# Scaling the half tiles between two layers on ScalarE instead of GpSimd, and holding their transposes back less

## The chip, the cores and the metric

One NeuronCore of a Trainium2 chip runs the kernel. The metric is device time in microseconds (us). The engines are named as in the profile: PE is TensorE, PEld its weight loads, DVE is VectorE, ACT is ScalarE, POOL is GpSimd, SP is the engine whose queue issues the DMAs.

## What is computed

Three steps in a row, all in float32 at the interface:

```
scores = (q @ k^T) / 8 * decay            # 4 x 8 heads, 576 positions, head size 64
x      = (scores @ v), laid out as 2304 x 512
P      = softmax-like gate of x, 8 rounds of row and column normalization (8 experts)
x      = sum over e of P[:, e] * (relu(x @ w1[e]) @ w2[e])       # 512 -> 1024 -> 512
h      = x @ w_in;  g = max(0.01 * h, h);  out = g @ w_out       # 512 -> 2048 -> 512
```

The matrices w_in and w_out arrive as 64-bit numbers and are turned into float32 on the chip.

## The kernel before, in words

Both feed-forward layers are cut into units of 512 hidden columns: 16 units for the eight experts (units 0 to 15), 4 for the second layer (units 16 to 19). Each unit runs over the tokens in three stages of 384 tokens per half (the 2304 tokens are two halves of 1152; tile j is 128 tokens, and tile j of the first half goes with tile j of the second; j runs from 0 to 8). Within a unit the product is done by a fast scheme of seven block products in place of eight, and each operand is a pair of 16-bit parts, high and low, so that three matmuls stand for one. The first products of a stage (`product_h`, L996) are interleaved by hand with the second products of an earlier stage (`group_s`, L1167; for units 0 and 15 the plain form, L1209). PE is given this order.

What the other engines do beside it is put in order while the program is built, by the class `Order`. It keeps a planned time `t` of PE and a planned time at which each engine comes free. Tasks stand in queues (evac, turn, gate, hid, weights, f64). After each few matmuls `tick` calls `pump`, which goes through the queues in this order and issues each task that is ready. A task with several engines ("AD": ACT or DVE) goes to the one that the plan has free the longest. The price of a task is `a + b * n` for n elements: on ACT 0.2 + 0.00089 n, on DVE 0.17 + 0.00105 n, on POOL 0.28 + 0.0020 n. `lat` is how long after the planned end of what it needs a task is held back:

```
L92   return (all(d.done is not None and d.done + x.lat <= self.t + 0.25 for d in x.deps)
L93           and (x.cond is None or x.cond()) and (not x.eng or min(self.free[e] for e in x.eng) <= self.t + SLACK))
```

The engines' own queues run in the order of issue; a task that the plan issues too early makes its engine wait on a semaphore, and with it all that is queued behind.

When a tile pair j of unit 15 is finished (`close`, L1190), it becomes an operand of the second layer; this is the turn (`turn_steps`, L1279). For each of the two half tiles (128 x 512) of the pair: a sum of absolute values (`sums`, L1289 on ACT or L1291 on DVE), then for both together a power of two for each row (`norms`, four small DVE instructions: L155, L156, L1299, L161), the scaling of the half tile in place by it (`scaled`, L1306), four PE transposes of 128 x 128 into a PSUM bank (`turned`, L1316), and a copy of that bank to SBUF on ACT or DVE (L63). `operand_tasks` then forms sums of blocks on POOL (`sums_a`, `sums_b`, L501 to L508), takes the 16-bit high parts (L63) and low parts (DVE, L530) and writes four pieces for each pair to DRAM from SP's queue (L455), from where the stages of the second layer load them into a ring (L479). There are 9 pairs, so 18 scalings, 72 transposes and 36 pieces.

In the same stretch the weights of units 16 and 17 are prepared: magnitudes (ACT, L197), high parts (ACT, L250 and L279), low parts and block differences (POOL, L260, L267, L285). The raw weights of the next unit (`load_raw`, L182) are asked for when the last of these is done and no piece is outstanding (`landed`, L173).

Of the kernel before, what the change touches and what calls it, by code (L numbers as in the profile page):

```python
# [13 lines left out]
AF = mybir.ActivationFunctionType  # L14
ALU = mybir.AluOpType
# [46 lines left out]
def copy_on(e, out_, in_):  # L62
    (e.copy if e is nc_of["A"] else e.tensor_copy)(out_, in_)  # L63
# [62 lines left out]
def retention_moe_ffn_kernel(ctx: ExitStack, tc: tile.TileContext, qk, vk, wg, wm, wf,  # L126
                             c_dt, c_gq, c_gk, c_id, out):
    nc = tc.nc
# [23 lines left out]
    def pow2(out_, in_, name):  # L152

        t = small.tile(list(out_.shape), F32, tag=f"pw{out_.shape[-1]}", name=f"pw{name}", bufs=2)
        nc.vector.tensor_scalar(t, in_, 2.0 ** -90, None, op0=ALU.max)  # L155
        nc.vector.tensor_scalar(out_.bitcast(I32), t.bitcast(I32), EXPM, EXPM,  # L156
                                op0=ALU.bitwise_xor, op1=ALU.bitwise_and)

    def recip2(out_, in_):

        nc.vector.tensor_scalar(out_.bitcast(I32), in_.bitcast(I32), -1.0, float(254 << 23),  # L161
                                op0=ALU.mult, op1=ALU.add)
# [394 lines left out]
    def idle_bank(name):  # L557

        return s1[1 - last_pair[0] % 2]
# [334 lines left out]
    y = [ypool.tile([P, DM], F32, name=f"y{i}") for i in range(2 * NJ)]  # L894
# [241 lines left out]
    def group_s(u, s, jj, what):  # L1136
# [53 lines left out]
        def close():  # L1190
            if jj == NT_S - 1:
                s_done.add((u, s))
            if u == NU1 - 1:
                turn_steps(s, j)
# [84 lines left out]
    def turn_steps(s, j0):  # L1279

        xs, st = {}, {}

        def sums(j, h):
            def f(e):
                if h == 0:
                    st["l", j] = small.tile([P, 2], F32, tag="l1", name=f"tl1{j}")
                i, o = y[h * NJ + j], st["l", j][:, h:h + 1]
                if e is nc.scalar:
                    nc.scalar.activation(junk, i, AF.Abs, accum_out=o)  # L1289
                else:  # L1290
                    nc.vector.tensor_reduce(o, i, axis=AX.X, op=ALU.add, apply_absolute_value=True)  # L1291
            return f

        def norms(j):
            def f():
                s1 = small.tile([P, 2], F32, tag="ts1", name=f"ts1{j}")
                s2 = st["s", j] = small.tile([P, 2], F32, tag="s2", name=f"ts2{j}")
                pow2(s1, st["l", j], f"t{j}")
                nc.vector.tensor_scalar(s2, s1, XS, None, op0=ALU.mult)  # L1299
                recip2(inv.rearrange("p (h j) -> p h j", h=2)[:, :, j], s1)  # L1300
            return f

        def scaled(j, h):
            def f():
                i = h * NJ + j
                nc.gpsimd.tensor_scalar(y[i], y[i], st["s", j][:, h:h + 1], None, op0=ALU.mult)  # L1306
            return f

        xt = [None, None]

        def turned(j, h):
            def f(e):
                i = h * NJ + j
                ptv = idle_bank(f"xt{i}").rearrange("p (k i) -> p k i", k=NP)
                for k in range(NP):
                    nc.tensor.transpose(ptv[:, k, :], y[i][:, 128 * k:128 * k + 128], ident)  # L1316
                xt[h] = wtmp.tile([P, NP, P], F32, tag="r64", name=f"tx{i}", bufs=R64)
                copy_on(e, xt[h], ptv)
            return f

        j, p, key = j0, turn_last, (1, s)

        def add(eng, n, f, deps, lat=LAT):
            x = Task(eng, n, f, tuple(d for d in deps if d), key, None, lat)
            order.queues["turn"].append(x)
            return x

        y_done = Task(None, 0, None, done=max(order.free["D"], order.free["A"]))
        a = [add("AD", 512, sums(j, h), (y_done,)) for h in range(2)]
        a = add("D", 300, norms(j), a)  # L1330
        b = [add("G", 512, scaled(j, h), (a,)) for h in range(2)]
        t = [add("AD", 512, turned(j, h), (b[h],) + p.get(f"x{h}", ()), 1.5) for h in range(2)]
        operand_tasks(1, j, xt, tuple(t), key, p)

    gates = []
# [160 lines left out]
```

## Time and profile before

| | |
|---|---|
| median of 3 runs | 1814.27 us (1813.0 to 1817.39) |
| profiled execution, span from first to last instruction | 1814.0 us |
| PE busy | 1780.4 us, 98% |
| DVE busy | 1484.6 us, 82% |
| ACT busy | 1260.0 us, 69% |
| POOL busy | 823.9 us, 45% |
| POOL, scaling of the half tiles (L1306) | 18 instructions, 33.3 us, from 1390 to 1486 us |

The profile is of one execution. A busy share is an average over the whole span; the turn takes place between about 1388 and 1500 us, and the rows of that stretch are what the change is read from. Small idle times of PE are listed in the trace by what ended them. Matmuls are pipelined, so a matmul row is longer than the distance to the next.

### The profile page before, as it was taken

To read this page: it belongs to the slowest core of one execution; us is meant where nothing else is said; L and a number is where in the kernel's file an instruction comes from. 1 tells how busy PE (TensorE), PEld (TensorE's weight loads), DVE (VectorE), ACT (ScalarE), POOL (GpSimd) and SP (SyncE) were. 2 spreads that over 40 slices of the span, in tenths; PEclk is the share of its full clock that TensorE was granted. 3 is DMA by queue.
4 is the path that set the end of the run, shared out by engine and by line. 5 is a ranking of instruction groups with operands and counts; after the bars stand their busy time and mean duration, and the time that the engine had idled before them with its cause. 6 is when DMAs were issued, how large, how long until landed. Compare 5 with 4: busy or idle time off the path is not lost.

```text
span 1814.0 us, 35903 instructions
## 1 busy us (share of the span) xinstructions
PE 1780.4 (98%) x13800; PEld 1294.5 (71%) x13800; DVE 1484.6 (82%) x2583; ACT 1260.0 (69%) x2657; POOL 823.9 (45%) x782
## 2 busy tenths in 40 slices
PE   8999999999999999999999999999999989999998
PEld 7755577777777777777777777777776556777776
DVE  7955989988888887888888888878875896788876
ACT  5776776767676677767676767777675667876753
POOL 4815452626344453626263444536234882443610
PEclk9999999999999999999999999999999999999999
DMA  9773445446354454454453544544443444435242
GB/s 339 272 250 102 144 139 169 141 137 186 112 172 126 147 161 137 133 171 133 139 186 107 176 124 154 163 132 133 152 129 114 160 156 146 129 104 159 79 128 82
DMA packets 206784, 272.99 MB, mean 150 GB/s; under 512 B 13698, under 2 KB 177556, under 8 KB 201492
## 3 DMA queue, kind: packets, MB, share of 16 engines
q1 hardware_dynamic: 206612, 270.70, 47.7%
q8 instruction: 108, 1.77, 0.4%
q14 instruction: 64, 0.52, 0.1%
HBM read 241.02 MB, written 29.63 MB: 149 GB/s over the span
## 4 chain that ended last, share of the span: by engine, by line
PE 89%; DVE 5%; DMA 2%; POOL 1%; ACT 1%; issue 1%; SPq 0%; DVEq 0%; POOLq 0%; ACTq 0%
PE s L1167 17%; PE hB L996 13%; PE hA L996 12%; PE hE L996 12%; PE s1a L1167 12%; PE s1b L1167 11%; PE hD L996 6%; PE s L1209 2%; DMA qk<-in_qk 1%; PE s1a L1209 1%; PE s1b L1209 1%; DVE xst L530 1%; DMA xring<-x 1%; POOL y L1306 1%; DVE hs L1087 0%
## 5 line engine op out<-in xcount | busy, mean ns | idle before, releaser
L996 PEld LDWEIGHTS <-w 128*128 128x128 f16 x5040 | 491.4, 98 | 260.9 <-issue 6.8
L1167 PEld LDWEIGHTS <-hs 128*128 128x128 f16 x3888 | 379.4, 98 | 88.5 <-DVE hs L1087 5.2
L260 POOL TENSOR_TENSOR w<-raw,w 128x384 f16<-128x384 f32 x152 | 168.8, 1128 | 384.7 <-ACT w L250 384.4
L1167 PEld LDWEIGHTS <-hp 128*128 128x128 f16 x2916 | 285.4, 98 | 79.9 <-issue 1.9
L267 POOL TENSOR_TENSOR raw<-raw 128x256 f32<-128x256 f32 x304 | 281.6, 926 | 19.9
L1180 DVE SCALAR_TENSOR_TENSOR y<-s,fac,y 128x256 f32<-128x256 f32 (+1 forms) x322 | 197.5, 614 | 105.9 <-PE s L1167 89.3
L996 PE MATMUL hE<-xring,w 128*128 128x384 f16 x1440 | 276.3, 327 | 3.4 <-POOL w L285 1.8
L996 PE MATMUL hB<-xring,w 128*128 128x384 f16 x1440 | 276.4, 327 | 0.4 <-ACT hB L1006 0.4
L996 PE MATMUL hA<-xring,w 128*128 128x384 f16 x1440 | 274.8, 327 | 0.0
L1167 PE MATMUL s<-w,hs 128*128 128x256 f16 x1932 | 263.7, 273 | 0.0
L1087 DVE TENSOR_TENSOR hs<-fs,hs 128x768 f16<-128x768 f32 (+1 forms) x228 | 240.3, 1057 | 7.4 <-ACT hs L1077 6.4
L285 POOL TENSOR_TENSOR w<-raw,w 128x512 f16<-128x512 f32 x148 | 201.9, 1379 | 72.6 <-ACT w L279 72.4
L1077 ACT ACTIVATE hs<-fs 128x768 f16<-128x768 f32 (+1 forms) x228 | 187.6, 823 | 46.8 <-DVE fs L1112 38.2
L415 POOL TENSOR_TENSOR f<-f,e 128x256 f32<-128x256 f32 x64 | 52.9, 826 | 343.3 <-DVE e L407 343.3
L1077 ACT ACTIVATE hp<-fp 128x384 f16<-128x384 f32 x240 | 160.6, 678 | 13.0 <-DVE fp L1035 12.0
L1180 DVE SCALAR_TENSOR_TENSOR y<-s1a,fac,y 128x256 f32<-128x256 f32 (+1 forms) x161 | 98.8, 614 | 59.0 <-ACT s L1185 32.8
L1167 PE MATMUL s1a<-w,hs 128*128 128x256 f16 x972 | 133.5, 273 | 4.6 <-ACT hs L1077 2.4
L996 PE MATMUL hD<-xring,w 128*128 128x384 f16 x720 | 136.8, 326 | 1.1 <-ACT hD L1024 1.1
L1180 DVE SCALAR_TENSOR_TENSOR y<-s1b,fac,y 128x256 f32<-128x256 f32 (+1 forms) x161 | 98.6, 613 | 46.8 <-PE s1b L1167 20.5
L1167 PE MATMUL s1b<-w,hs 128*128 128x256 f16 x960 | 132.2, 274 | 2.3 <-DVE hs L1087 1.9
L1167 PE MATMUL s1a<-w,hp 128*128 128x256 f16 x972 | 132.6, 273 | 1.0 <-DVE y L1180 1.0
L1167 PE MATMUL s<-w,hp 128*128 128x256 f16 x966 | 131.8, 273 | 0.0
(213 smaller groups left out, 2683.0 us busy)
## 6 DMA issues: line engine op xcount, KB each, us to landing
xring<-x SPq DMA_DIRECT2D x413, 384.0 KB
raw<-in_wm SPq DMA_DIRECT2D x32, 1024.0 KB
r<-in_wf SPq DMA_DIRECT2D x64, 256.0 KB
qk<-in_qk SPq DMA_DIRECT2D x16, 512.0 KB
vk<-in_vk SPq DMA_DIRECT2D x16, 512.0 KB
wf_s<-f SPq DMA_DIRECT2D x32, 256.0 KB
raw<-wf_s SPq DMA_DIRECT2D x8, 1024.0 KB
x<-xst SPq DMA_DIRECT2D x30, 256.0 KB
```

The costliest lines, as they stand in the source:

```text
L260: nc.gpsimd.tensor_tensor(v[0], v[1], v[2], op=ALU.subtract)
L267: nc.gpsimd.tensor_tensor(o, x, y_, op=ALU.subtract)
L285: (nc.gpsimd if u or part else nc.vector).tensor_tensor(lo, r, hi, op=ALU.subtract)
L415: nc.gpsimd.tensor_tensor(dst, dst, cur["tx"].bitcast(F32), op=ALU.mult)
L530: nc.vector.tensor_tensor(st[d][:, :, 1], src[d](), st[d][:, :, 0], op=ALU.subtract)
L996: nc.tensor.matmul(bank, w[:, a, wi, k, :], x[:, :, b, k, :], start=r in (1, 5) and k == q == 0, stop=k == 1 and q == 2, skip_group_check= ...
L1077: nc.scalar.activation(hid[k][:, 0, a:b], src[:, a:b], AF.Relu if moe and relu else AF.Copy)
L1087: nc.vector.tensor_tensor(t[:, 1, a:b], src[:, a:b], t[:, 0, a:b], op=ALU.subtract)
L1167: nc.tensor.matmul(out_, t[:, a, i, ts], w[:, b, wi, 0, :], start=start and k == 0, stop=k == 5, skip_group_check=True)
L1180: nc.vector.scalar_tensor_tensor(out_, bank, f, out_, op0=ALU.mult, op1=ALU.add)
L1209: nc.tensor.matmul(bank, t[:, a, i, ts], w[:, b], start=l == g == q == 0, stop=l == g == 1 and q == 2, skip_group_check=True)
L1306: nc.gpsimd.tensor_scalar(y[i], y[i], st["s", j][:, h:h + 1], None, op0=ALU.mult)
```

## The change

The scaling of a half tile is issued on ACT (an activation "copy" with a factor for each partition) instead of POOL, and the plan books it on ACT at 0.656 us instead of on POOL at 1.304 us. The transposes of a half tile are held back 0.5 us instead of 1.5 us after the planned end of the scaling. Nothing else is edited; but since the order of all later tasks follows from the plan, other tasks can change their place or their engine.

```diff
         def scaled(j, h):
             def f():
                 i = h * NJ + j
-                nc.gpsimd.tensor_scalar(y[i], y[i], st["s", j][:, h:h + 1], None, op0=ALU.mult)
+                nc.scalar.activation(y[i], y[i], AF.Copy, scale=st["s", j][:, h:h + 1])
             return f
...
         a = add("D", 300, norms(j), a)
-        b = [add("G", 512, scaled(j, h), (a,)) for h in range(2)]
-        t = [add("AD", 512, turned(j, h), (b[h],) + p.get(f"x{h}", ()), 1.5) for h in range(2)]
+        b = [add("A", 512, scaled(j, h), (a,)) for h in range(2)]
+        t = [add("AD", 512, turned(j, h), (b[h],) + p.get(f"x{h}", ()), 0.5) for h in range(2)]
         operand_tasks(1, j, xt, tuple(t), key, p)
```

## Rows read from the trace of the kernel before

**Rows 1.** Page, part 1: busy time, share of the span, instructions of each engine.

```profile
PE 1780.4 (98%) x13800; PEld 1294.5 (71%) x13800; DVE 1484.6 (82%) x2583; ACT 1260.0 (69%) x2657; POOL 823.9 (45%) x782
```

**Rows 2.** Windows: stretch, length, busy us (instructions) by engine, granted clock, DMA.

```profile
800.00:1380.00 580.00, 580.00 (x4426) 431.42 (x4425) 480.81 (x832) 410.11 (x861) 254.91 (x243) 1.00 0.47 143
1380.00:1541.00 161.00, 149.64 (x911) 90.52 (x910) 129.07 (x214) 105.71 (x224) 105.00 (x94) 0.98 0.47 151
```

**Rows 3.** PE's waits, 1380 to 1540 us: total us, times, longest us.

```profile
PE s1a L1167 <- ACT hs L1077: 2.2, 1, 2.2
PE s1a L1316 <- POOL y L1306: 2.0, 3, 1.7
PE hE L996 <- POOL w L285: 1.8, 2, 1.0
PE s1a L1167 <- DVE hs L1087: 1.5, 1, 1.5
PE s1b L1316 <- POOL y L1306: 1.2, 1, 1.2
PE hD L996 <- ACT hD L1024: 1.1, 1, 1.1
```

**Rows 4.** Windows of the turn, the two stretches at the lower clock last.

```profile
1388.00:1500.00 112.00, 103.66 (x598) 59.71 (x596) 95.99 (x160) 72.39 (x156) 88.95 (x78) 0.98 0.48 160
1440.00:1487.00 47.00, 40.11 (x227) 22.10 (x226) 44.79 (x71) 29.54 (x61) 45.09 (x40) 0.99 0.53 177
...
1486.50:1489.90 3.40, 3.40 (x15) 2.24 (x14) 3.40 (x7) 2.21 (x5) 0.00 (x0) 0.53 0.21 75
...
1537.30:1541.00 3.70, 3.70 (x17) 2.40 (x18) 2.69 (x3) 1.70 (x4) 3.33 (x4) 0.54 0.00 0
```

**Rows 5.** Groups on POOL, 1388 to 1500 us: busy us, mean ns, idle before.

```profile
L1306 POOL TENSOR_SCALAR y<-y,ts 128x512 f32<-128x512 f32 x18 | 33.3, 1860 | 7.8 <-DVE inv L161 6.1 <-ACT w L279 1.1 <-DVE ts L1299 0.4
```

**Rows 6.** Groups on ACT, 1388 to 1500 us.

```profile
L63 ACT COPY tx<-s1b 128x512 f32<-128x512 f32 x7 | 4.1, 586 | 4.5 <-PE s1b L1316 4.4
...
L63 ACT COPY tx<-s1a 128x512 f32<-128x512 f32 x6 | 3.5, 585 | 5.9 <-PE s1a L1316 5.9
...
L235 ACT ACTIVATE raw<-raw,sw 128x512 f32<-128x512 f32 x4 | 2.9, 721 | 0.0
```

**Rows 7.** Timeline of DVE: the last norms before the scaling, of three pairs.

```profile
1426.16 0.17 DVE L1299 TENSOR_SCALAR ts<-ts 128x2 f32<-128x2 f32 x1
...
1436.52 0.17 DVE L1299 TENSOR_SCALAR ts<-ts 128x2 f32<-128x2 f32 x1
...
1462.74 0.58 DVE L1299 TENSOR_SCALAR ts<-ts 128x2 f32<-128x2 f32 x1
```

**Rows 8.** Timeline of PE: the first transposes of the same three pairs.

```profile
1428.28 0.60 PE L1316 MATMUL s1a<-ident,y 128*128 128x128 f32 x4
...
1438.58 0.60 PE L1316 MATMUL s1b<-ident,y 128*128 128x128 f32 x4
...
1465.11 0.66 PE L1316 MATMUL s1b<-ident,y 128*128 128x128 f32 x4 [1.24 <-POOL y L1306]
```

**Rows 9.** Timeline of POOL: one pair's scalings.

```profile
1401.34 4.17 POOL L1306 TENSOR_SCALAR y<-y,ts 128x512 f32<-128x512 f32 x2 [1.20 <-DVE inv L161]
```

**Rows 10.** Groups on DVE, 1388 to 1500 us.

```profile
L530 DVE TENSOR_TENSOR xst<-sa,xst 128x512 f16<-128x512 f32 x9 | 8.1, 905 | 0.0
L530 DVE TENSOR_TENSOR xst<-tx,xst 128x512 f16<-128x512 f32 x9 | 8.0, 893 | 0.0
L530 DVE TENSOR_TENSOR xst<-sb,xst 128x512 f16<-128x512 f32 x9 | 7.3, 809 | 0.1
...
L63 DVE COPY tx<-s1a 128x512 f32<-128x512 f32 x3 | 2.1, 692 | 2.2 <-PE s1a L1316 2.2
```

**Rows 11.** Timeline of DVE while the scalings of Rows 9 ran.

```profile
1402.14 0.68 DVE L530 TENSOR_TENSOR xst<-sb,xst 128x512 f16<-128x512 f32 x1
```

**Rows 12.** Timeline of SP's queue: the load of unit 17's second raw weights.

```profile
1481.66 0.40 SPq L182 DMA_DIRECT2D raw<-wf_s  x1
```

## The prediction

> **What bounds the kernel now.** I read first the page's busy times: PE is busy 98% of the span [rows 1], so only what lets PE stand, or slows its clock, can be won. Next the windows, to see where PE stands: from 800 to 1380 us it never does; in the 161 us from 1380 to 1541, which hold the turn and its aftermath, it is busy 149.6 us, so it stands for 11.4 us [rows 2]. In two places there its granted clock is at half (1.2 GHz instead of 2.4): 3.4 us after the stand at 1482 to 1486, and about 3.4 us after the one at 1535 to 1537 [rows 4]. Half speed for 3.4 us costs 1.7 us each time. Together 11.4 + 3.4 = 14.8 us are all that this stretch can give back, 0.8% of the span.
>
> Then PE's waits in that stretch [rows 3], for who ends the stands. Only 2.0 + 1.2 = 3.2 us end with the instruction that the change moves (POOL's scaling, L1306). 2.2 + 1.5 = 3.7 us end with the high and low parts of the hidden values of unit 16 (ACT and DVE), 1.8 us with a weight part on POOL, 1.1 us with ACT's copy to hD.
>
> Last the windows and groups of the turn, to see which engine is behind. From 1440 to 1487 us DVE is busy 44.8 of 47 us and POOL 45.1, ACT only 29.5 [rows 4]. So two engines are full there, not one. POOL has 33.3 us of scalings among 89.0 us of work from 1388 to 1500 [rows 4, 5]; DVE has none.
>
> **The change, part by part.** The sum is made against the profiled execution, 1814.0 us from first to last instruction; the median of the runs is 0.3 us above it, which I add at the end.
>
> *The scaling itself.* Removed from POOL: 18 instructions of 1.86 us, 33.3 us [rows 5]. Added to ACT: 18 of the nearest form in this stretch, the scaling of raw weights (L235), same shape, types and a factor for each partition: 0.72 us [rows 6], 18 x 0.72 = 13.0 us, which lifts ACT from 72.4 to 85.4 of 112 us. For a pair, norms to scaled tiles falls from 3.7 us (4.2 where both stand in a row, [rows 9]) to 1.4.
>
> *The transposes.* In the plan the first scaling of a pair ends 1.30 - 0.66 = 0.65 us earlier and the hold is 1.0 us shorter, so they stand 1.65 us earlier in PE's queue; the second half's 2 x 0.65 + 1.0 = 2.3 us earlier. The scaled tile is really there 1.86 - 0.72 = 1.1 us earlier for the first, 2.3 for the second. So the second keep their distance, but the first lose 0.5 us of it: PE is asked earlier than the data come. What then counts is DVE, whose norms come before the scaling. In the third pair from [rows 7, 8] PE comes to the transposes at 1463.87 (1465.11 less its 1.24 us idle), 0.55 us after the norms ended (1462.74 + 0.58 = 1463.32); in the other two 1.95 and 1.89 us after. Of the nine pairs these three are the tightest; the others have 2.4 us or more in the same views. Less 1.65, that is 0.30, 0.24 and -1.10 us, where 0.8 is needed (0.72 and two hand-overs). PE would wait 0.5, 0.6 and 1.9, together 3.0 us; with 0.3 us in ACT's queue for each, 3.9. This replaces 3.2 us. Term: +0.7 us. Bounds: -3.2 (all waits gone, if DVE gets ahead) and +8.5 (all of the last six pairs as the tightest: 6 x 1.95 = 11.7, less 3.2).
>
> *The wait added on ACT.* ACT now waits for DVE's norms; POOL did so for 6.1 us [rows 5]. Behind a waiting scaling stand ACT's evacuations of the first products (hB, p, u, fp, hD), and behind them PE. Today ACT has a third of its time free and PE waits 1.1 us for such a copy [rows 3]. Lower bound 0, upper bound all the added 13.0 us; I take 0.8 us, near the one wait that the rows show. Term: +0.8.
>
> *The wait for hD.* The 1.1 us [rows 3] stand at the end of a stretch of the chain of waits: scalings until 1405.5 [rows 9], transposes, their copy, four block sums on POOL, a cast on ACT that waits for them, and behind it in ACT's queue the copy to hD. With the scalings done about 2.8 us earlier the chain ends before PE asks. Term: -1.1; bounds -1.1 and 0.
>
> *The end of the turn.* The 3.7 us for the hidden values of unit 16, with 1.7 us of clock behind them, come from DVE, which is still busy with the pieces. Does the change unload DVE? Two things oppose. (1) Copies: with ACT booked for the scaling just before, the plan sends more "AD" work to DVE. Now ACT makes 7 + 6 = 13 of the 18 copies of transposes [rows 6] and DVE 5; I expect some five more on DVE, at 0.69 us each [rows 10]: +3.5 us. (2) DVE's instructions are longer while POOL works: the 27 wide low parts mean 0.87 us [rows 10], against 0.68 for one that ran beside a scaling without loss [rows 11]. Under the scalings of [rows 9] there is none of that excess, over all of the stretch it is 0.19 us a low part; I estimate about 0.35 us for a pair, so 9 x 0.35 = 3 us go with the scalings. (1) and (2) cancel; what remains is that each pair's pieces begin 1 to 2 us earlier, so less of the last two pairs lies in front of the hidden values. I take half of the 3.7: -1.8, and keep the clock drop. Bounds: -5.4 (stand and clock both gone) and +3.5 (the copies come, the relief does not).
>
> *The weights of unit 17.* Their second raw load is issued at 1481.66 us [rows 12], behind the writes of the pieces in SP's queue, which wait for DVE, and after unit 16's last weight parts on POOL, between the scalings. A POOL freed of 33.3 us ends those sooner; the 36 piece writes move up with the pairs, by 1 to 2 us. The load then starts a little earlier, and the 1.8 us wait for L285 shrinks. Term: -0.9 (half); bounds -3.5 (wait and clock drop gone) and 0.
>
> Sum: +0.7 + 0.8 - 1.1 - 1.8 - 0.9 = -2.3 us, so 1811.7; with the 0.3 us to the median **1812 us**.
>
> One rule of the Trainium skill bears on (2). "SBUF — State Buffer", section "Who interferes with whom", says that a DVE instruction with two SBUF inputs and a GpSimd one that reads SBUF exclude each other for a whole instruction. By it taking scalings off POOL would free DVE more than the 3 us; the trace disagrees in part: the low part of [rows 11] has two SBUF inputs and ran at its shortest in the middle of the scalings of [rows 9]. What it would give is the first rival.
>
> **Rivals.** *DVE comes free.* The 27 wide low parts last 8.1 + 8.0 + 7.3 = 23.4 us [rows 10]; at 0.68 they would last 18.4, so 5 us of DVE are lost to POOL in these alone, and half as much again in the narrow ones and the norms would make about 8. If most of it went with the scalings, DVE would be ahead by the end: the 3.2, the 3.7 with 1.7 of clock, and the 1.1 would go, less 0.8 on ACT: 8.9 us, 1805. For it: DVE and POOL are both full from 1440 to 1487 [rows 4]. Against: the rest of POOL's work, 55.6 of 89.0 us, stays, and DVE's excess is small under the scalings.
>
> *PE is asked too early: slower.* The place is PE's queue in front of the transposes of the last six pairs; the price is the difference between when DVE's norms are ready and when PE arrives, now without the 1.65 us. It decides from the point where the mean wait for a pair exceeds 3.2 / 9 = 0.36 us. If DVE lags in each of the last six pairs as it does in the tightest, PE waits 11.7 instead of 3.2 us, a third clock drop adds 1.7, and none of the later terms comes: 1814.3 + 8.5 + 1.7 = 1824. For it: DVE is 95% busy there [rows 4], and further copies may go to it. Against: each stand of PE lets DVE catch up, and two of the three tightest pairs were 1.9 us clear [rows 7, 8].
>
> *The waits change only their name.* Scaling and transposes shift together, the copies sent to DVE eat the rest, and the end of the turn is as late: +0.7 + 0.8 - 1.1 = +0.4, so 1814 to 1815.
>
> **How the numbers follow.** Forecast 0.42 (its own range 1808 to 1816), DVE free 0.23, too early 0.18, only the name 0.17. A measurement of this kernel can tell about 0.3%, 5.4 us, from no change: 1808.8 and 1819.7. Faster has the first rival and 0.05 of the forecast's lower edge: 0.28. Slower is the second rival, 0.18. The rest, 0.54, is the same. The range leaves out a tenth at each side: down to 1804, just under the first rival; up to 1821, about two thirds of the way to the second.
>
> **What would show it.** Right: the waits for L1306 stand under ACT with 3 to 5 us; DVE stays over 90% busy in the second half of the turn; POOL has some 33 us less there, ACT 12 to 14 more; about half the transposes' copies are on DVE; the 1.1 us for hD is gone; the stand at 1482 us is there, but under 3 us. Wrong to the fast side: DVE's wide low parts near 0.7 us, no stand and no clock drop at the end. Wrong to the slow side: waits for the scaling above 8 us, or evacuations on ACT (L1006 to L1024) late behind a scaling that waits for DVE. If PE stands somewhere outside 1380 to 1560 us where it does not now, the plan has changed more than I assume.

## The result and the profile after

The kernel after takes 1830.38 us (median of 4 runs, 1829.72 to 1830.72) beside 1814.81 for the kernel before on the same chip: ratio 1.0086, 95% interval [1.0071, 1.010]. It is slower by 15.6 us, where I had forecast 2 us faster; the time lies above my range. The profiled execution spans 1828.9 us, against 1814.0.

Part 1 of the page, as in [rows 1]:

```profile
PE 1783.0 (97%) x13800; PEld 1294.9 (71%) x13800; DVE 1489.3 (81%) x2585; ACT 1269.1 (69%) x2677; POOL 791.7 (43%) x764
```

PE has as many instructions as before and 2.6 us more busy time; the other 12.3 us are idle time. The windows of after (stretch, length, then busy us of PE, PEld, DVE, ACT, POOL; granted clock, DMA share, GB/s):

```profile
800.00:1380.00 580.00, 580.00 (x4428) 431.63 (x4427) 481.26 (x833) 410.49 (x862) 254.34 (x243) 1.00 0.47 143
1380.00:1560.00 180.00, 157.75 (x943) 94.21 (x942) 134.02 (x217) 118.02 (x251) 75.35 (x78) 0.95 0.43 135
1388.00:1500.00 112.00, 98.78 (x535) 54.59 (x534) 94.06 (x153) 73.72 (x157) 54.19 (x56) 0.96 0.47 152
1440.00:1487.00 47.00, 40.80 (x220) 22.43 (x221) 42.25 (x62) 32.49 (x73) 27.96 (x29) 0.96 0.44 147
```

and the second stretch in the trace of before:

```profile
1380.00:1560.00 180.00, 167.65 (x1047) 103.66 (x1046) 139.09 (x231) 122.71 (x257) 109.27 (x99) 0.98 0.46 146
```

From 800 to 1380 us nothing differs [rows 2]. In the 180 us that follow PE is busy 9.9 us less, at a lower mean clock. POOL did lose its scalings (88.95 to 54.19 us in the turn, [rows 4]). ACT gained only 1.3 us there, not 13: it gave copies away, and others of its instructions fall behind 1500 us.

Who took the copies is seen in the groups of after, 1388 to 1500 us (as [rows 5, 6, 10]):

```profile
L1306 ACT ACTIVATE y<-y,ts 128x512 f32<-128x512 f32 x18 | 12.3, 714 | 7.7 <-DVE ts L1299 7.7
L530 DVE TENSOR_TENSOR xst<-tx,xst 128x512 f16<-128x512 f32 x8 | 8.9, 1116 | 0.0
L530 DVE TENSOR_TENSOR xst<-sa,xst 128x512 f16<-128x512 f32 x8 | 8.4, 1054 | 0.0
L530 DVE TENSOR_TENSOR xst<-sb,xst 128x512 f16<-128x512 f32 x8 | 6.5, 807 | 0.1
L63 DVE COPY tx<-s1b 128x512 f32<-128x512 f32 x6 | 4.2, 692 | 6.9 <-PE s1b L1316 6.8
L63 DVE COPY tx<-s1a 128x512 f32<-128x512 f32 x6 | 4.1, 689 | 5.1 <-PE s1a L1316 3.2 <-ACT w L279 1.9
```

Twelve of the transposes' copies are on DVE; before it had five. In front of these twelve DVE stands for 6.9 + 5.1 = 12.0 us, mostly until PE's transposes are done. Before it stood 5.1 us in front of its five, 2.2 for the three in [rows 10] and 2.9 for the other two:

```profile
L63 DVE COPY tx<-s1b 128x512 f32<-128x512 f32 x2 | 1.4, 691 | 2.9 <-ACT p L1010 1.5 <-PE s1b L1316 1.3
```

In return DVE has two of the sums (L1291, 0.67 us each) instead of six. And its wide low parts did not get shorter without the scalings beside them: (8.9 + 8.4 + 6.5) / 24 = 0.99 us, against 0.87. In this window there are 24 of them instead of 27: the last pair's pieces fall behind 1500 us. (All 27 take 26.4 us, before 23.5.) The delay is plainest in SP's queue, before (first fence; start, us, instructions merged) and after:

```profile
1488.42 10.20 SPq L455 DMA_DIRECT2D x<-xst  x6
1498.72 31.46 SPq L479 DMA_DIRECT2D xring<-x  x14
```

```profile
1488.11 0.38 SPq L182 DMA_DIRECT2D raw<-wf_s  x1
1494.24 13.64 SPq L455 DMA_DIRECT2D x<-xst  x4
1508.05 0.53 SPq L479 DMA_DIRECT2D xring<-x  x1
1509.75 0.32 SPq L455 DMA_DIRECT2D x<-xst  x1
1510.18 5.19 SPq L479 DMA_DIRECT2D xring<-x  x7
```

The last piece (L455) leaves 11 us later, at 1509.75 instead of 1498.3. PE's waits of after, 1380 to 1560 us, answer to [rows 3]:

```profile
PE s1b L1316 <- ACT y L1306: 4.1, 2, 2.9
PE s1a L1167 <- ACT hs L1077: 3.2, 1, 3.2
PE s1a L1316 <- ACT y L1306: 3.2, 3, 1.7
PE hE L996 <- ACT w L279: 2.9, 1, 2.9
PE s1b L1167 <- DVE hs L1087: 1.8, 1, 1.8
PE hA L996 <- ACT w L250: 1.2, 1, 1.2
PE hE L996 <- DMA xring<-x: 1.2, 1, 1.2
...
PE hA L996 <- POOL w L260: 0.9, 1, 0.9
PE hA L996 <- DMA xring<-x: 0.7, 1, 0.7
PE s1a L1167 <- DVE hs L1087: 0.6, 1, 0.6
```

Three things grew: the scalings (7.3 us, 3.2 before), the hidden values of unit 16 (5.6, 3.7 before), the weights of unit 17 (L250, L260, L279 and 0.4 on L285: 5.4, 1.8 before); the ring loads (1.9) are new, and the 1.1 us for hD is gone. Behind the stands the clock is at 0.50 for longer, 17.0 us in three stretches instead of 6.8 in two [rows 4]:

```profile
1466.20:1469.60 3.40, 2.73 (x10) 1.88 (x11) 2.38 (x4) 3.17 (x6) 0.00 (x0) 0.50 0.93 251
1493.50:1500.30 6.80, 5.85 (x25) 3.73 (x24) 3.74 (x10) 4.32 (x10) 0.00 (x0) 0.50 0.11 40
1548.10:1554.90 6.80, 3.84 (x14) 1.72 (x15) 2.97 (x3) 3.85 (x8) 5.46 (x7) 0.50 0.00 0
```

PE was busy for 12.4 us of them, against 7.1 before; half of the difference, 2.7 us, is the cost. PE's order of products (L996, L1167, L1209) is the same in every kernel here, so the same product can be found in two traces. Its **lag** is its start less its start before, less that difference for the product at 1381.5 us, where the change has not begun. In after the lag is +5.7 at the product that started at 1486.5 us in before, +8.8 at 1502, +10.8 at 1532 (the first of unit 17), +14.6 at 1542 and +14.5 at 1599: 5.7 us in the turn, 5.1 at its end, 3.8 at unit 17's weights, nothing later. Stands of PE from the product at 1381.5 to the one at 1599 are 23.6 us against 12.8, so idle time makes 10.9 of it, the clock some 2.7.

### The profile page after: what moved, and what is told of

The parts are those of the page before. It is cut to its first block, busy times and chain, and to the rows that moved or that the text cites. A ratio compares the mean times of both kernels' runs of the same rounds, so it can differ in the third digit from the quotient of the medians.

```text
span 1828.9 us, 35900 instructions
## 1 busy us (share of the span) xinstructions
PE 1783.0 (97%) x13800; PEld 1294.9 (71%) x13800; DVE 1489.3 (81%) x2585; ACT 1269.1 (69%) x2677; POOL 791.7 (43%) x764
## 4 chain that ended last, share of the span: by engine, by line
PE 89%; DVE 6%; ACT 1%; issue 1%; DMA 1%; POOL 1%; SPq 0%; DVEq 0%; ACTq 0%; POOLq 0%
PE s L1167 17%; PE hB L996 12%; PE hE L996 12%; PE hA L996 12%; PE s1a L1167 11%; PE s1b L1167 11%; PE hD L996 6%; PE s L1209 2%; PE s1a L1209 1%; DVE xst L530 1%; PE s1b L1209 1%; DMA xring<-x 1%; DVE hs L1087 0%; DVE hp L1087 0%; PE s1b L211 0%
## 5 line engine op out<-in xcount | busy, mean ns | idle before, releaser
L996 PEld LDWEIGHTS <-w 128*128 128x128 f16 x5040 | 490.8, 98 | 267.5 <-issue 6.5
L1167 PEld LDWEIGHTS <-hs 128*128 128x128 f16 x3888 | 379.4, 98 | 90.5 <-DVE hs L1087 5.1
L1167 PEld LDWEIGHTS <-hp 128*128 128x128 f16 x2916 | 285.7, 98 | 80.8 <-issue 2.7
L260 POOL TENSOR_TENSOR w<-raw,w 128x384 f16<-128x384 f32 x152 | 167.4, 1118 | 396.4 <-ACT w L250 396.0
L267 POOL TENSOR_TENSOR raw<-raw 128x256 f32<-128x256 f32 x304 | 281.2, 925 | 19.9
L996 PE MATMUL hE<-xring,w 128*128 128x384 f16 x1440 | 277.1, 328 | 6.9 <-DMA xring<-x 3.6
L996 PE MATMUL hA<-xring,w 128*128 128x384 f16 x1440 | 274.3, 326 | 2.7 <-ACT w L250 1.2
L996 PE MATMUL hB<-xring,w 128*128 128x384 f16 x1440 | 275.4, 326 | 1.6 <-ACT hB L1006 1.0
L1167 PE MATMUL s<-w,hs 128*128 128x256 f16 x1932 | 264.2, 273 | 0.9 <-ACT s L1185 0.9
L1087 DVE TENSOR_TENSOR hs<-fs,hs 128x768 f16<-128x768 f32 (+1 forms) x228 | 238.8, 1050 | 7.3 <-ACT hs L1077 6.3
L285 POOL TENSOR_TENSOR w<-raw,w 128x512 f16<-128x512 f32 x148 | 202.1, 1380 | 67.2 <-ACT w L279 67.0
L1077 ACT ACTIVATE hs<-fs 128x768 f16<-128x768 f32 (+1 forms) x228 | 187.5, 823 | 45.5 <-DVE fs L1112 37.8
L1077 ACT ACTIVATE hp<-fp 128x384 f16<-128x384 f32 x240 | 160.6, 678 | 13.2 <-DVE fp L1035 12.1
L1167 PE MATMUL s1a<-w,hs 128*128 128x256 f16 x972 | 133.4, 273 | 4.8 <-ACT hs L1077 3.5
L996 PE MATMUL hD<-xring,w 128*128 128x384 f16 x720 | 136.8, 326 | 0.0
L1167 PE MATMUL s1b<-w,hs 128*128 128x256 f16 x960 | 131.8, 273 | 3.0 <-DVE hs L1087 2.6
L1167 PE MATMUL s1a<-w,hp 128*128 128x256 f16 x972 | 133.3, 274 | 1.0 <-DVE y L1180 1.0
L1167 PE MATMUL s<-w,hp 128*128 128x256 f16 x966 | 131.8, 273 | 0.0
```

Of the source, the lines that this page charges most:

```text
L260: nc.gpsimd.tensor_tensor(v[0], v[1], v[2], op=ALU.subtract)
L267: nc.gpsimd.tensor_tensor(o, x, y_, op=ALU.subtract)
L285: (nc.gpsimd if u or part else nc.vector).tensor_tensor(lo, r, hi, op=ALU.subtract)
L996: nc.tensor.matmul(bank, w[:, a, wi, k, :], x[:, :, b, k, :], start=r in (1, 5) and k == q == 0, stop=k == 1 and q == 2, skip_group_check= ...
L1077: nc.scalar.activation(hid[k][:, 0, a:b], src[:, a:b], AF.Relu if moe and relu else AF.Copy)
L1087: nc.vector.tensor_tensor(t[:, 1, a:b], src[:, a:b], t[:, 0, a:b], op=ALU.subtract)
```

## Experiments

All are variants of the two kernels. "Booked" is the engine on which the plan puts the scaling; in e3, e7, e8, e10, e15 and e18 it still says GpSimd (1.30 us) while the instruction runs on ACT. "Weights first" is the edit of e9. "Last piece" is the start of the last L455, shifted like the lags. Each ratio is against the kernel before as measured beside that run (medians of 1814.5 to 1815.5 us).

The theories, by the letters that the expectations use: A, the hold is too short and TensorE is asked too early; B, the plan, which now books the scaling on ACT, sends copies to DVE; C, ACT waits for the norms and holds up its queue; D, unit 17's second raw load is late; E, any new order costs about 10 us; F, the order misses slots for unit 17's weights; G, the loss is in the turn itself; J, A in the turn and F behind it; B2, booking the scalings on ACT itself harms the turn.

| run | runs on / booked | hold | weights first | median us | ratio, 95% | last piece | lag 1487 | lag 1532 | lag 1599 |
|---|---|---|---|---|---|---|---|---|---|
| before | POOL/POOL | 1.5 | - | 1814.8 | 1 | 1498.3 | 0 | 0 | 0 |
| after | ACT/ACT | 0.5 | - | 1830.4 | 1.0086 [1.0071, 1.010] | 1509.3 | +5.7 | +10.8 | +14.5 |
| e1 | ACT/ACT | 1.5 | - | 1830.0 | 1.0080 [1.0065, 1.0095] | 1506.0 | +2.4 | +13.4 | +16.0 |
| e2 | POOL/POOL | 0.5 | - | 1826.3 | 1.0060 [1.0045, 1.0075] | 1501.2 | +4.7 | +7.4 | +10.9 |
| e3 | ACT/POOL | 1.5 | - | 1812.9 | 0.9984 [0.9975, 0.9994] | 1496.7 | -1.4 | -1.8 | -3.5 |
| e4 | as after, copies on ACT | 0.5 | - | 1823.5 | 1.0041 [1.0027, 1.0055] | 1499.5 | 0.0 | +6.5 | +8.5 |
| e5 | as after, load freed | 0.5 | - | 1828.6 | 1.0077 [1.006, 1.0094] | 1509.6 | +6.8 | +10.8 | +14.3 |
| e6 | POOL/POOL | 2.0 | - | 1825.9 | 1.0061 [1.0046, 1.0076] | 1503.6 | +1.8 | +6.0 | +9.7 |
| e7 | ACT/POOL | 0.5 | - | 1823.2 | 1.0045 [1.003, 1.006] | 1498.7 | +1.8 | +3.2 | +8.0 |
| e8 | as e3, load freed | 1.5 | - | 1813.6 | 0.9994 [0.9985, 1.0003] | 1496.7 | -1.4 | -1.6 | -3.3 |
| e9 | ACT/ACT | 0.5 | yes | 1825.2 | 1.0058 [1.0041, 1.0075] | 1507.1 | +5.9 | +7.0 | +9.5 |
| e10 | ACT/POOL | 1.5 | yes | 1810.7 | 0.9975 [0.9966, 0.9984] | 1495.7 | -2.9 | -1.2 | -5.9 |
| e11 | ACT/ACT | 1.5 | yes | 1826.6 | 1.0063 [1.0048, 1.0078] | 1510.9 | +3.1 | +14.0 | +9.3 |
| e12 | POOL/POOL | 1.5 | yes | 1813.3 | 0.9991 [0.9982, 1.0] | 1497.7 | -0.3 | +1.3 | -3.4 |
| e13 | ACT/ACT | 0.25 | - | 1827.5 | 1.0072 [1.0057, 1.0087] | 1512.3 | +8.7 | +12.7 | +12.0 |
| e14 | ACT/ACT | 0.75 | - | 1832.8 | 1.0103 [1.0086, 1.012] | 1516.1 | +7.7 | +18.2 | +16.5 |
| e15 | ACT/POOL | 2.0 | yes | 1812.3 | 0.9988 [0.9978, 0.9997] | 1498.0 | -0.2 | -0.4 | -3.0 |
| e16 | ACT/ACT | 2.5 | - | 1834.0 | 1.0107 [1.0092, 1.0122] | 1506.9 | -2.0 | +14.7 | +16.9 |
| e17 | ACT/ACT | 2.5 | yes | 1822.1 | 1.0038 [1.0023, 1.0052] | 1503.7 | +2.1 | +9.3 | +6.7 |
| e18 | ACT/POOL | 0.5 | yes | 1818.8 | 1.0027 [1.0017, 1.0036] | 1498.9 | +1.6 | +5.6 | +3.1 |

**The parts of the change (e1 to e4).** e1 is after with `1.5` for `0.5`; e2 is before with `0.5` for `1.5`; e3 and e4, against after:

```diff
e3
-        b = [add("A", 512, scaled(j, h), (a,)) for h in range(2)]
+        b = [add("G", 512, scaled(j, h), (a,)) for h in range(2)]
-        t = [add("AD", 512, turned(j, h), (b[h],) + p.get(f"x{h}", ()), 0.5) for h in range(2)]
+        t = [add("AD", 512, turned(j, h), (b[h],) + p.get(f"x{h}", ()), 1.5) for h in range(2)]
e4
-        t = [add("AD", 512, turned(j, h), ...
+        t = [add("A", 512, lambda j=j, h=h: turned(j, h)(nc.scalar), ...
```

> Scaling on ACT, hold back at 1.5 us. Theory A (PE is asked too early: the shorter hold makes it): PE's waits for the scaling fall from the 7.3 us of the changed kernel to under 2, the time to 1812 to 1818 us. Theory B (the plan, which books the scaling on ACT, sends the copies of the transposes to DVE, and DVE is the late engine): still about 10 of 18 copies on DVE, time 1822 to 1830. Theory C (ACT, waiting for DVE's norms, holds up what is queued behind it): time 1822 to 1830 too, with ACT's waits before the scaling still at 5 us or more.

> Scaling on POOL as before, only the hold shortened to 0.5 us. Theory A: each first transpose comes 1.0 us earlier, and PE's waits for the scaling rise from 3.2 to some 10 us; time 1820 to 1826. Theories B and C: the engine makes the loss, so the time stays at 1814 to 1819.

> Scaling runs on ACT, but the plan books it on POOL as before, hold 1.5 us: all instructions keep the order they had before, only the engine that scales differs. Theory A: PE's waits for the scaling go to under 1 us, hD's wait goes; time 1809 to 1814. Theory B: the same, since the copies stay where they were: 1809 to 1814. Theory C: ACT waits for the norms and what is behind it is late: 1818 to 1828.

> The changed kernel (ACT, hold 0.5 us), but all 18 copies of the transposes on ACT, which takes some 12 x 0.69 = 8 us off DVE in the turn. Theory B: DVE's norms come earlier, PE's waits for the scaling fall to 3 us or less, time 1812 to 1818. Theory A: the hold is as short as before, the waits stay at 5 to 8 us, time 1823 to 1830. Theory C: ACT still fuller, 1828 to 1836.

Measured: of the four only e3 is faster. It issues PE, DVE and SP in the order of before, and the scalings run on ACT at 0.72 us, waiting for the norms as they would in after. So the engine is not the harm, and ACT's added wait isn't either, on balance: PE's waits for the scaling (3.2 us before) are gone, 3.4 us of waits for ACT's copies of the transposes stand in their place (0.4 before), and from 1381 to 1599 us there is one half-clock stretch instead of two. Together it gains 0.16% [0.06, 0.25]. Its low parts on DVE, in the same order and without the 33 us of POOL beside them, take 24.4 us for 27:

```profile
L530 DVE TENSOR_TENSOR xst<-tx,xst 128x512 f16<-128x512 f32 x9 | 9.2, 1024 | 0.0
L530 DVE TENSOR_TENSOR xst<-sa,xst 128x512 f16<-128x512 f32 x9 | 8.6, 953 | 0.0
L530 DVE TENSOR_TENSOR xst<-sb,xst 128x512 f16<-128x512 f32 x9 | 6.6, 730 | 0.1
```

0.90 us each, 0.87 before [rows 10]: the scalings on POOL had not been what stretches them. Two of them from e3's timeline, the first with nothing on POOL beside it, the second under POOL's differences of weights (L285, L267):

```profile
1449.52 0.68 DVE L530 TENSOR_TENSOR xst<-sa,xst 128x512 f16<-128x512 f32 x1
...
1459.76 1.64 DVE L530 TENSOR_TENSOR xst<-sa,xst 128x512 f16<-128x512 f32 x1
```

So it is in every kernel here: of the wide low parts that overlap nothing on POOL none takes more than 0.69 us. In before, seven overlap scalings alone (mean 0.75 us) and sixteen overlap one of POOL's two-input instructions, block sums and weight parts (mean 0.97). Of the 5.1 us above 0.68, 0.5 go with the seven and 4.6 with the sixteen, and those POOL instructions stayed: seventeen overlap them in e3 (1.03), eighteen in after (1.13). By the rule of the Trainium skill's "SBUF — State Buffer", section "Who interferes with whom", that I had weighed, the low parts should have been shorter without the scalings; the trace disagrees for these, and agrees for POOL's two-input instructions.

The new booking with the old hold costs about as much as the whole change (e1 1.0080, after 1.0086), and the new hold alone costs 11 us (e2, with 8.5 us of waits for the scaling, near what A had forecast). C falls with e3, and A, as the whole cause, with e1. In e4 the last piece leaves at 1499.5, the waits for the scaling are 2.4 us and the lag at 1502 us is +1.8 instead of +8.8. So the copies that the plan sent to DVE hold up the end of the turn, as B has it, with one reserve: the plan of e4 draws an order of its own, too. Its time misses B's 1812 to 1818, for it loses 4.9 + 2.0 + 1.1 us at the weights of unit 17, for which ACT, now with all copies, is late.

**The raw load, the longer hold, the engine in a second order (e5 to e8).** e5 (of after) and e8 (of e3) drop `cond=landed` from the task that asks for the raw weights; e6 is before with hold 2.0; e7 is e3 with hold 0.5, which gives PE, DVE and SP the order of e2.

> The changed kernel, but the raw weights of the next unit no longer wait until no piece is outstanding. Theory D (a large part of the loss is not at the transposes but 60 us later, where unit 17's weights are late because their second raw load is issued at 1488 instead of 1482 us behind the pieces): the load is issued before 1482, PE's waits for unit 17's weights (L250, L260, L279, L285; 5.3 us) and the 6.8 us of half clock go, time 1822 to 1826. Without D: 1828 to 1833.

> The kernel before with the hold at 2.0 instead of 1.5 us: the opposite direction, POOL scales. Theory A (a shorter hold asks PE too early): waits for the scaling fall below 3.2 us, time 1811 to 1815. Theory E (the order before fits by luck, and any new order of the turn costs some 10 us at its end, whatever the direction): time 1821 to 1830, with the weights of unit 17 late again.

> The order of the kernel with POOL and a hold of 0.5 us (1826.3 us), but scaled on ACT. If the engine alone helps, as in the old order (-2.5 us), PE's waits for the scaling fall from 8.5 to 4 us or less and the time to 1819 to 1824. If ACT's waits for DVE's norms take it back (theory C): 1825 to 1829.

> ACT scales in the order of the kernel before (1812.9 us), and the raw weights no longer wait for outstanding pieces. Theory D: unit 17's weights come in time, the 1.8 us wait for L285 and the clock drop at 1535 go: 1808 to 1812. Theory E (any new order costs): 1816 to 1826.

In e5 the load of unit 17's second raw weights is issued at 1475 instead of 1488 us, and the waits at unit 17's first products stay: the load is not the cause, and D falls; e8 is no faster than e3. e7 against e2 repeats e3 against before in another order: ACT is some 3 us better. e6 costs 11 us though its hold is longer: a short hold is not needed for a loss.

**Unit 17's weights (e9 to e12).** The kernels after, e3, e1 and before, each with:

```diff
-                order.queues["weights"] += [x for x in w_all if x.key[0] == u + 1]
+                for x in w_all:
+                    if x.key[0] == u + 1:
+                        order.queues["gate" if u == NU1 and x.key[1:] == ("w1", 0) else "weights"].append(x)
...
     def need(key):
-        order.flush("weights", lambda k: k == key)
+        for q in ("gate", "weights"):
+            order.flush(q, lambda k: k == key)
```

The reason is in ACT's timeline, the high parts of unit 17's first weights (L250). Before:

```profile
1522.23 0.50 ACT L250 CAST w<-raw 128x384 f16<-128x384 f32 x1
1523.52 0.50 ACT L250 CAST w<-raw 128x384 f16<-128x384 f32 x1
1533.67 1.13 ACT L279 CAST w<-raw 128x512 f16<-128x512 f32 x2
```

After:

```profile
1534.72 0.50 ACT L250 CAST w<-raw 128x384 f16<-128x384 f32 x1
1544.88 0.51 ACT L250 CAST w<-raw 128x384 f16<-128x384 f32 x1
1549.98 1.14 ACT L279 CAST w<-raw 128x512 f16<-128x512 f32 x2 [4.59 <-POOL raw L267]
```

The queue of weights is served after three others and in turns with that of the hidden values. In after the first L250 comes 12 us later, the second 10 us behind it; between them ACT makes the hidden values of unit 16 (L1077) and copies PSUM banks; then L260, L267, L279 and L285 follow in one piece while PE stands.

> The kernel after; the only edit: the tasks that prepare the first weight matrix of unit 17 (key (17, w1, 0)) wait in the gate queue, which is empty by then and is served before the hidden values, instead of the weights queue, which is served last; need() flushes both. Theory F (the loss is where the kernel's own order misses slots on ScalarE for unit 17's weights: in the kernel after, the second high part loses every slot to the hidden values of unit 16's last stage, and the whole chain behind it is forced in a row when TensorE is already there; the kernel's own planned end is 1724.6 before, 1735.2 after, and 1727.2 with this edit): about 1822 (1820 to 1825); the waits at unit 17's first products (1.2 on L250, 0.9 on L260, 2.9 on L279, 0.4 on L285) fall to under 2.5 together, and the L250 pair of unit 17 lies within 3 us of each other. Theory G (the loss is in the turn itself, in the later transposes and norms; unit 17 only pays what came from there): 1828 to 1831, and the time moves from the weights to the next wait.

> As e3 (scalings on ScalarE, but booked as GpSimd with the old hold: the order of before) with the edit of e9. Theory F: the kernel's own planned end falls from 1724.6 to 1717.5, so about 1807 (1804 to 1810), faster than both kernels; the 1.8 us wait on L285 at unit 17's first products goes, and so does part of the waits of unit 17's later parts. Theory G: 1812 to 1814, no difference from e3.

> As e1 (the kernel after with the old hold of 1.5) with the edit of e9. Theory F: e1 stood at 1830.0 with a planned end of 1735.4; with the edit it is 1722.4, so 1816 to 1820: the new order of the turn then costs no more than 3 us against before. Theory G: 1828 to 1831, as e1.

> The kernel before with the edit of e9 alone (scalings on GpSimd; order of PE, DVE and SP as in e10). Theory F: 1814.8 less the same 5 to 7 us as e10 against e3, so 1808 to 1811; e10 is then 1 to 3 us faster than this, by the engine alone, as e3 is than before. Theory G: 1814 to 1816.

The planned end is what the kernel's own planner has for PE's time when it has issued everything. In e9 the pair comes together,

```profile
1531.09 0.51 ACT L250 CAST w<-raw 128x384 f16<-128x384 f32 x1
1532.18 0.50 ACT L250 CAST w<-raw 128x384 f16<-128x384 f32 x1
1540.76 1.14 ACT L279 CAST w<-raw 128x512 f16<-128x512 f32 x2
```

of the weights' waits only 2.2 us (L285) are left, and the time falls by 5.2 us. That is a third of the loss; the time lies just above what F had forecast. In before and in e3, where these weights were nearly in time, the edit gives some 2 us, not the 5 to 7 of F; in e11 it gives 3.4 us, where the planned end fell by 13. The lag at 1487, +5.9, is not touched, as G had it. Both were half right.

**Which orders lose in the turn (e13 to e18).** e13, e14 and e16 are after with holds of 0.25, 0.75 and 2.5; e17 is e16 with the edit of e9; e15 and e18 are that edit on e3's booking, with holds of 2.0 and 0.5.

> The kernel after with a hold of 0.25 instead of 0.5: one number, in the same direction as the change went. In the kernel's own plan this gives another order whose planned end is 1725.1, where the kernel after has 1735.2 and the kernel before 1724.6; unit 17's weights are ready in time in it. Theory F, widened (what counts is where the order that the planner draws leaves a chain unserved, above all unit 17's weights; hold and engine act only through that order): 1816 to 1821, some 10 us faster than after. Theory A (the hold is too short, TensorE is asked too early): slower than after, 1831 to 1834. Theory E (any new order costs about 10 us): 1826 to 1831.

> The kernel after with a hold of 0.75: planned end 1726.2. Theory F: 1817 to 1822, 9 us faster than after, though e1 with a hold twice as long was not faster. Theory A: 1827 to 1829, a quarter of the way back. Theory E: 1826 to 1831.

> Scalings on ScalarE, booked as GpSimd, hold 2.0, with the edit of e9 (unit 17's first weights served before the hidden values): planned end 1717.9, as e10 (1717.5) by another order. Without the edit this hold has a planned end of 1732.1, and its counterpart with the scalings on GpSimd (e6) ran at 1825.9. Theory F: 1809 to 1815, no slower than before. Theory E: 1822 to 1826.

> The kernel after with a hold of 2.5: between the planned end of the norms and the transposes lie 0.66 + 2.5 = 3.16 us, where before has 1.30 + 1.5 = 2.80, e1 0.66 + 1.5 = 2.16 and after 1.16. Over the runs so far the lag against before at 1487 us falls with this lead: +8.7 at 0.91, +5.7 at 1.16, +2.4 at 2.16, and 0 or below at 2.80 and 3.30 on ScalarE. Theory J (two causes: the lead sets the turn, the weights of unit 17 the rest): the lag at 1487 is +1 or less, the waits on L1306 fall below 1 us; the weights are late in this plan (planned end 1735.6), so the end is still +8 to +12 and the time 1823 to 1827. Theory B2 (booking the scalings on ScalarE is itself the harm in the turn, by crowding its slots): lag at 1487 +2.5 or more, as e1, and the time 1828 to 1831.

> e16 with the edit of e9 (unit 17's first weights served before the hidden values). Theory J: with both causes mended 1814 to 1818, the weights' waits below 2 us, lag at 1487 +1 or less. Theory B2: 1821 to 1826, as e9 and e11.

> e7 (scalings on ScalarE, booked as GpSimd, hold 0.5: lead 1.80) with the edit of e9. e7 ran at 1823.2, +1.8 at 1487 and +6.2 more by 1542. Theory J: the +1.8 stays, the later part falls to +1 or less: 1815 to 1818. If the weights matter only together with the old hold: 1821 to 1824.

e13 and e14 refute the widened F: their plans end where that of before does, and on the chip they are 13 and 18 us slower. E falls with e15: e6's order, with its weights mended and the scalings on ACT, is 0.12% [0.03, 0.22] faster than before. J is right in the turn of e16 and wrong in the sum; in e17 it misses both (lag +2.1, 1822.1 us, where B2 had 1821 to 1826), and e18 lies 1 us above its range. B2 fails in e16, whose lag it had at +2.5 or more. In e16 the waits for scalings are all but gone, the lag at 1487 is -2.0, and then (PE's waits, 1380 to 1560 us):

```profile
PE hA L996 <- DMA xring<-x: 9.1, 1, 9.1
PE hA L996 <- ACT w L250: 4.5, 1, 4.5
PE hE L996 <- ACT w L279: 2.0, 1, 2.0
...
PE s1b L1316 <- ACT y L1306: 0.8, 1, 0.8
```

with SP's queue behind it:

```profile
1487.78 19.64 SPq L455 DMA_DIRECT2D x<-xst  x8
1507.52 22.47 SPq L479 DMA_DIRECT2D xring<-x  x9
```

The last pair's pieces are nearly as late as in after (1506.9 and 1509.3), so here the longer hold only moves the stand from the transposes to the ring load. The late last piece goes with the booking over all of the kernels. Booked on POOL, on either engine, 5 or 6 copies are on DVE and the last piece leaves between 1495.7 and 1503.6 us. Booked on ACT, 8 to 14 copies are on DVE and it leaves between 1503.7 and 1516.1, whatever the hold (but for e4, whose copies are forced to ACT). Booking changes the engine and the price in the plan together; the two were not tried apart. Hold for hold, with the scalings on ACT each time, the booking costs about 17 us at 1.5 (e1, e3) and 7 at 0.5 (after, e7); with the weights first about 16 (e11, e10) and 6 (e9, e18). The short hold costs about 10 us under the old booking (e7 against e3; some 8 with the weights first) and nothing under the new one. Why e6 with its hold of 2.0 is 5 us later with the last piece than before is left open. The fastest is e10, the scalings on ACT with the old booking, the old hold and the weights first: 0.25% [0.16, 0.34] faster than before, and about 20 us below after. The copies on ACT and the weights first in one kernel, the two repairs of after, were not tried together.

## Why the prediction was wrong

**The scaling itself**: right. 0.714 us each (forecast 0.72), POOL 34.8 us less in the turn. **The wait added on ACT** (+0.8): right in size. ACT stood 7.7 us before the scalings, but only 0.5 us of PE's waits after show evacuations late behind it (hB). In e3 ACT stands 7.1 us, and the price is seen elsewhere, at the copies of the transposes (3.4 us). **hD** (-1.1): the wait is gone in after, but not by my chain: in e3, where the scalings are done earlier and the order is as before, it stays at 1.1 us. What e3 measures, about -2 us, is near my sum of -2.3 by chance: there the waits for the scaling, hD and L285 are -3.2, 0 and 0, and the clock stretch at 1537 us, which my sum had kept, is gone.

**The transposes** (+0.7): too small. The waits are 7.3 us, not 3.9, with one more stretch at half clock. I moved three pairs by 1.65 us and took DVE's norms as standing still. In after the last pair's norms end at 1494.7 us instead of 1480.1, for in DVE's queue they now stand behind the hidden values of unit 16 (L1087). Before:

```profile
1479.51 0.57 DVE L1299 TENSOR_SCALAR ts<-ts 128x2 f32<-128x2 f32 x1
...
1484.93 2.23 DVE L1087 TENSOR_TENSOR hs<-fs,hs 128x768 f16<-128x768 f32 x2
```

After:

```profile
1491.55 1.90 DVE L1087 TENSOR_TENSOR hs<-fs,hs 128x768 f16<-128x768 f32 x2
...
1494.50 0.17 DVE L1299 TENSOR_SCALAR ts<-ts 128x2 f32<-128x2 f32 x1
```

**The end of the turn** (-1.8) is the step that failed: the lag grows by 5.1 us there. It says "(1) and (2) cancel", copies against relief. The copies came, seven instead of five, 7 x 0.69 = 4.8 us; the relief did not (0.90 us in e3, 0.99 in after, against (23.4 - 3) / 27 = 0.76 in the forecast). It could not: the low part of [rows 11] had shown that a scaling does not stretch it, and I still gave the scalings 3 of the 5 us. "Each pair's pieces begin 1 to 2 us earlier" turned into the last piece 11 us later. I had the bound in hand (+3.5, "the copies come, the relief does not") and sized it as engine time only. DVE was 95% busy in the second half of the turn [rows 4] and each pair passes through it three times, for the norms, the copies and the low parts, among the hidden values of unit 16. The work itself is the smaller part: with four sums fewer (2.7 us) less than half of the 4.8 us is left. What grew is DVE's standing in front of copies, 12.0 us against 5.1, the wide low parts, by 2.9 us, and the place of the last norms in its queue. That the copies are at the root is what e4 shows, for all of them together, in an order of its own (it takes five off DVE that before had there, too). How the 11 us split over these stays open, and in e16, where DVE stands only 3.7 us in front of eight copies, why the last piece is late is not shown.

**The weights of unit 17** (-0.9): wrong in sign, +3.6 us of waits and 3.4 us more of half clock. I looked at the load and at POOL; the raw load did come later (1488.11, [rows 12]) but does not matter (e5). What matters is ACT's order near 1525 to 1545 us, which I had not read: it is a product of the plan, and the plan had changed by then. e9 shows this as 5.2 us.

Of the rivals, "PE is asked too early" came nearest: its place, PE's queue before the transposes, has the waits, and 1824 is nearer than 1812. "DVE comes free" falls with the low parts. The price of "too early" was to be 8.5 + 1.7 us there, of which 4.1 of wait and one 3.4 us clock stretch are found, and its remedy fails: e16, with a long hold, has hardly any of these waits and is the slowest of all. That the plan might change more than I assumed stood in the prediction only as stands outside 1380 to 1560 us, where hardly anything changed; inside it, it had no case and no chance in the sum.

## What to carry to other kernels

When a program's order is drawn by a planner, an edit to a cost, an engine or a delay is first of all a new order: build the variant that changes the engine and keeps the old order (e3) before arguing about either. Price moved flexible work (here 7 copies) at the engine that closes the chain, at its busiest stretch, not at its mean load, and with the time that this engine will stand for the work's input. And when a wait is removed and the time stays, ask whether the last item of the stage leaves earlier; here its start (L455) went with the lag at 1532 us over nearly all of the kernels.

## What was not expected of the hardware

DVE's wide low parts (two SBUF inputs, 128 x 512) gained nothing when 33 us of GpSimd scalings left their stretch: 0.87 us before, 0.90 in e3 in the same order. They take 0.67 to 0.69 us with nothing on GpSimd beside them, and 0.97 to 1.13 in the mean (before, e3, after) where they overlap one of its two-input instructions. Half-clock stretches of 6.8 us occur, and of 10.2 in e1, e7 and e11, where before has only 3.4; e12, the only one with none between 1381 and 1599 us, has 13.1 us of stands there, more than the 11.7 of e3, which has one stretch of 3.4 us. And a `tensor_scalar` of 128 x 512 in float32 with a factor for each partition takes 1.86 us on GpSimd and 0.714 us on ScalarE.
